# The second product of a packed-attention and FFN kernel by one level of Strassen's scheme, in two phases over the inner layer

## The chip, the cores and the metric

The kernel runs on one core of a Trainium2 chip. The metric is the device time of one execution in microseconds; three executions of the kernel before took 696.87, 698.0 and 700.45 us, median 698.0.

## What is computed

```python
def _attn_ref(q, k, v, p):              # 8 batches, 8 heads, 576 tokens, 64 wide; 32 packed queries p
    ...
    p_packed = sm_attn(p, k, v)         # attention of the 32 packed queries over the 576 tokens
    out = sm_attn(q, p_packed, p_packed)  # attention of every token over the 32 packed rows
def _moe_ref(x, w_in, w_out):           # x: 4608 x 512, w_in: 512 x 2048, w_out: 2048 x 512
    h = x @ w_in
    g = h * (1.0 / (1.0 + np.exp(-1.702 * h)))
    return g @ w_out
```

All inputs and the output are f32. The output of the attention, heads side by side, is the x of the second function.

## The kernel before, in words

The attention weights of a token over the 32 packed rows, times (packed rows x `w_in`), are the first product h, so x itself is never formed. For each batch, `m_chunk` multiplies the packed rows by a chunk of 512 columns of `w_in` (f32, four chunks); `h_mm` multiplies the result, as stationary blocks of 128 columns, by the attention weights of half a batch (288 tokens). `out_mm` is the second product g @ `w_out`: for one block f of 128 inner columns, and one block i of 128 tokens, it adds to a PSUM bank of 128 tokens x 512 output columns. There are 16 blocks f and four token blocks in a batch; the 64 tokens left over in each batch are kept (`h_over`) and done for two batches at once (`over_mm`).

Both products want more digits than one fast (fp32r) matmul gives. Each operand is split into an upper part (a cast to fp32r: `m_upper`, `a_upper`, `h_upper`, `upper_w`) and a lower part (what is left: `m_lower`, `a_lower`, `h_lower`, `lower_w`), and three terms are added: upper x upper, upper x lower, lower x upper. So a block of h is six matmuls of 288 columns (`h_mm`, line 605), a block of the second product three of 512 (`product`, line 665):

```python
def product(acc, g, f, at, start, stop):
    for i, (part, gp) in enumerate(((0, g[0]), (1, g[0]), (0, g[1]))):
        nc.tensor.matmul(
            acc, gp[:, at : at + P], wo[f][:, part, :],
            start=(start and i == 0), stop=(stop and i == 2),
        )
```

The gate between them is a Tanh on ScalarE (`h_tanh`, line 613) and a multiplication on VectorE (`h_gate`, `h_over`, line 595). Tanh and the Exp of the two softmaxes are in one activation table. Weights arrive as words of eight bytes and are decoded by ScalarE (`begin_w`, line 208) and VectorE (`join_w`, line 220).

The order of the work is a table of steps, `order`, written out by hand: its entries run from first to last, and each engine executes its own instructions in that order. Waits between engines are by semaphores that the tile framework sets. Short `warm` matmuls on an identity stand in the table where TensorE has no work in the first microseconds. SP's queue issues nearly all transfers, in the table's order.

Of the kernel before, what the change touches and what calls it, by code (L numbers as in the profile page):

```python
# [8 lines left out]
F32 = mybir.dt.float32  # L9
# [12 lines left out]
def kernel(  # L22
# [42 lines left out]
    NF = DF // P  # L65
    FC = 512
    NFC = DF // FC
    CF = FC // P
    NB = S // P
    REST = S - NB * P  # L70
    KC = (S + P - 1) // P
    KLAST = S - (KC - 1) * P
    DEC = 3
    MB = 2
    LATE = [(B - 1, 2)]
# [6 lines left out]
    ps_b = ctx.enter_context(tc.tile_pool(name="ps_b", bufs=2, space=PSUM))  # L82
# [7 lines left out]
    w_in_sb = [cst.tile([P, NP, FC], F32, name=f"w_in{i}") for i in range(NFC)]  # L90
    w_in_raw = w_in.bitcast(U16)
    w_out_raw = w_out.bitcast(U16)

# [9 lines left out]
    def o_tile(name):  # L103
        return wk.tile([P, DM], F32, tag="o", name=name, bufs=4)

    def bank_b(name):
        return ps_b.tile([P, FC], F32, tag="psb", name=name)

    def bank_h(name):
        return ps_h.tile([P, FC], F32, tag="psh", name=name)  # L110

    def bank_acc(i):
        return lambda name: ps_acc.tile([P, FC], F32, tag=f"acc{i}", name=name)
# [7 lines left out]
    def warm(i, n):  # L121

        t = ps_h.tile([P, FC], F32, tag="psh", name=f"warm{i}")
        for _ in range(n):
            nc.tensor.matmul(t[:, :P], ident, ident, start=True, stop=True)  # L125
# [5 lines left out]

    kq = {}


# [23 lines left out]

    slot = [12, 4, 8, 12]
    queue = []
    for c in range(NFC):
        queue += [("in", c, j) for j in range(NP)]
        queue += [("out", i) for i in range(CF * c, CF * (c + 1))]
    raw = {}
    wo = {}

    def slot_of(w):  # L170
        return slot[w[1]] + w[2] if w[0] == "in" else w[1]


    def columns(part):
        return slice(0, FC) if part is None else slice(part * FC // 2, (part + 1) * FC // 2)

    def load_w(n, part=None):
        w = queue[n]
        i = slot_of(w)
        if w[0] == "in":  # L180
            src = w_in_raw[w[2] * P : (w[2] + 1) * P, 4 * w[1] * FC : 4 * (w[1] + 1) * FC]
        else:
            src = w_out_raw[w[1] * P : (w[1] + 1) * P, :]
        if not part:
            raw[i] = wk.tile([P, DM, 2], U32, tag=f"wo{i}", name=f"raw{i}")
        halves = raw[i].rearrange("p n w -> p (n w)").bitcast(U16)
        at = columns(part)
        a, e = 4 * at.start, 4 * at.stop - 1
        nc.sync.dma_start(halves[:, a:e], src[:, a + 1 : e + 1])

    tops = wk.tile([P, 4, DM], U32, tag="late", name="tops")
    tops = [tops[:, i, :] for i in range(4)]
    for t in tops:  # L200
        nc.gpsimd.memset(t, 0)
    dec = {}
    top = {}

    def begin_w(n, part=None):
        top[n, part] = tops[(n + (part or 0)) % 4]
        at = columns(part)
        nc.scalar.copy(  # L208
            top[n, part].bitcast(F16).rearrange("p (n h) -> p n h", h=2)[:, at, 1],
            raw[slot_of(queue[n])].bitcast(BF16).rearrange("p n (w h) -> p n w h", h=2)[:, at, 1, 0],  # L210
        )

    def join_w(n, part=None):
        w = queue[n]
        at = columns(part)
        if w[0] == "in":
            dec[n] = w_in_sb[w[1]][:, w[2], :]
        else:
            dec[n] = wk.tile([P, DM], F32, tag="dec", name="dec", bufs=DEC)
        nc.vector.scalar_tensor_tensor(  # L220
            dec[n][:, at].bitcast(U32), raw[slot_of(w)][:, at, 0], 13, top[n, part][:, at],
            op0=ALU.logical_shift_right, op1=ALU.bitwise_or,
        )

    def upper_w(n, engine=nc.scalar):
        i = slot_of(queue[n])
        wo[i] = wk.tile([P, 2, DM], F32R, tag=f"wo{i}", name=f"wo{i}")
        move(engine, wo[i][:, 0, :], dec[n])

    def lower_w(n, engine=nc.gpsimd):  # L230
        w = wo[slot_of(queue[n])]
        engine.tensor_tensor(w[:, 1, :], dec[n], w[:, 0, :].bitcast(F32), op=ALU.subtract)

    def lower_w_mm(n, bank):

        st["wl", n] = bank = bank(f"pswl_{n}")
        nc.tensor.matmul(bank, ident, dec[n], start=True, stop=False)
        nc.tensor.matmul(bank, minus, wo[slot_of(queue[n])][:, 0, :], start=False, stop=True)

    def lower_w_copy(n, engine=nc.scalar):  # L240
        move(engine, wo[slot_of(queue[n])][:, 1, :], st["wl", n])

    st = {}

# [10 lines left out]
    def new1(b, eo):  # L258
        st["x", 1, b, eo] = x_tile(f"x1_{b}_{eo}")
        st["mx", 1, b, eo] = wk.tile([P, 2], F32, tag="mx1", name=f"mx1_{b}_{eo}", bufs=2)  # L260

    def scores1_first(half):

        for eo in range(2):
            if half == 0:
                new1(0, eo)
            st["bank", eo, half] = (bank_acc(half) if eo else bank_b)(f"ps1_0_{eo}_{half}")
        for j in range(NP):
            for eo in range(2):
                mm1(0, eo, half, st["bank", eo, half], j)  # L270

    def max1_first(eo, half):
        nc.vector.tensor_reduce(
            st["mx", 1, 0, eo][:, half : half + 1], st["bank", eo, half][:, :NH],
            axis=AX.X, op=ALU.max,
        )

    def scores1_mm(b, half, banks=(bank_b, bank_b)):
        if half == 0:
            for eo in range(2):  # L280
                new1(b, eo)
# [29 lines left out]
    def exp1_first(eo, half):  # L311
# [3 lines left out]
            st["x", *key][:, tokens(half)], st["bank", eo, half][:, :NH], AF.Exp,  # L315
# [17 lines left out]


# [18 lines left out]
    def turn1_last_mm(b):  # L353
        st["bank", "t", b] = bank = bank_b(f"pstl_{b}")
# [13 lines left out]

    dram = ctx.enter_context(tc.tile_pool(name="dram", bufs=1, space=bass.MemoryType.DRAM))
# [1085 lines left out]
```

## Time and profile before

| what | value |
|---|---|
| median of three runs | 698.0 us |
| the profiled execution | 697.0 us, its span (first to last instruction; nothing lies around it) |
| PE (matmul) busy | 688.2 us, 5032 instructions |
| PEld (weight load) busy | 562.6 us, 5032 instructions |
| DVE (VectorE) busy | 437.2 us, 1112 instructions |
| ACT (ScalarE) busy | 261.9 us, 628 instructions |
| POOL (GpSimd) busy | 86.3 us, 106 instructions |
| mean granted TensorE clock | 0.994 of full speed |
| moved by DMA | 65.18 MB, 94 GB/s over the span |

The profile gives busy time as the union of an engine's instructions. Matmuls are pipelined, and one that lasts 0.396 us may be followed by the next after 0.231 us, so the pace is read from starts, not from durations. An f32 matmul of the program stands in the profile as two. A load of the stationary operand (PEld) belongs to each matmul.

### The profile page before, as it was taken

To read this page: it belongs to the slowest core of one execution; us is meant where nothing else is said; L and a number is where in the kernel's file an instruction comes from. 1 tells how busy PE (TensorE), PEld (TensorE's weight loads), DVE (VectorE), ACT (ScalarE), POOL (GpSimd) and SP (SyncE) were. 2 spreads that over 40 slices of the span, in tenths; PEclk is the share of its full clock that TensorE was granted. 3 is DMA by queue.
4 is the path that set the end of the run, shared out by engine and by line. 5 is a ranking of instruction groups with operands and counts; after the bars stand their busy time and mean duration, and the time that the engine had idled before them with its cause. 6 is when DMAs were issued, how large, how long until landed. Compare 5 with 4: busy or idle time off the path is not lost.

```text
span 697.0 us, 12983 instructions
## 1 busy us (share of the span) xinstructions
PE 688.2 (99%) x5032; PEld 562.6 (81%) x5032; DVE 437.2 (63%) x1112; ACT 261.9 (38%) x628; POOL 86.3 (12%) x106
## 2 busy tenths in 40 slices
PE   8999999999999999999999999999999999999997
PEld 5688788788888888887888878887888887878885
DVE  2998884536565467555685467775785647855443
ACT  4788544423324323433223233332232333333220
POOL 1431372112300224111000000000000000000000
PEclk8999999999999999999999999999999999999999
DMA  8998603342101612055000613034200160010001
GB/s 306 369 346 253 264 1 107 77 128 77 65 1 21 192 39 80 16 130 185 1 31 2 158 46 141 16 97 123 95 16 1 28 186 1 11 51 1 1 15 61
DMA packets 55260, 65.18 MB, mean 94 GB/s; under 512 B 35808, under 2 KB 40864, under 8 KB 54176
## 3 DMA queue, kind: packets, MB, share of 16 engines
q1 hardware_dynamic: 55120, 64.23, 28.9%
q8 instruction: 40, 0.66, 0.4%
q14 instruction: 20, 0.16, 0.1%
q10 hardware_dynamic: 80, 0.13, 0.0%
HBM read 50.78 MB, written 13.57 MB: 92 GB/s over the span
## 4 chain that ended last, share of the span: by engine, by line
PE 95%; DVE 1%; issue 1%; DMA 1%; POOL 0%; ACT 0%; POOLq 0%; DVEq 0%
PE acc L665 52%; PE h L605 29%; PE acc_over L665 5%; PE psm_None L437 4%; PE ps L495 2%; PE pspv L408 1%; PE ps L250 1%; DMA q<-q 1%; PE warm L125 1%; DVE w_in L220 0%; DVE xt L551 0%; DVE sm L539 0%; PE pspt L427 0%; DVE sm L540 0%; DVE x L506 0%
## 5 line engine op out<-in xcount | busy, mean ns | idle before, releaser
L665 PE MATMUL acc<-wo,ghi 128*128 128x512 f32 x1024 | 322.8, 396 | 0.0
L665 PEld LDWEIGHTS acc<-wo,ghi 128*128 128x128 f32 x1024 | 180.1, 188 | 40.0 <-issue 10.3
L613 ACT ACTIVATE g<-h 128x288 f32<-128x288 f32 x256 | 104.1, 410 | 274.7 <-PE h L605 258.8
L665 PE MATMUL acc<-wo,glo 128*128 128x512 f32 x512 | 202.0, 395 | 0.0
L595 DVE SCALAR_TENSOR_TENSOR g<-g,h 128x288 f32<-128x288 f32 (+1 forms) x256 | 104.8, 415 | 116.8 <-ACT g L613 116.2
L605 PE MATMUL h<-ahi,mhi 128*128 128x288 f32 x496 | 139.9, 297 | 0.2 <-DVE g L595 0.2
L605 PE MATMUL h<-ahi,mlo 128*128 128x288 f32 x496 | 138.8, 295 | 0.0
L665 PEld LDWEIGHTS acc<-wo,glo 128*128 128x128 f32 x512 | 96.2, 188 | 22.6 <-DVE glo L592 0.3
L605 PEld LDWEIGHTS h<-ahi,mhi 128*128 128x128 f32 x496 | 93.2, 188 | 16.4 <-DVE x L506 4.9
L605 PE MATMUL h<-alo,mhi 128*128 128x288 f32 x496 | 105.1, 293 | 0.0
L605 PEld LDWEIGHTS h<-ahi,mlo 128*128 128x128 f32 x496 | 93.3, 188 | 6.9
L592 DVE TENSOR_TENSOR glo<-g,ghi 128x288 fp32r<-128x288 f32 (+1 forms) x190 | 79.3, 428 | 14.8 <-ACT ghi L117 10.8
L605 PEld LDWEIGHTS h<-alo,mhi 128*128 128x128 f32 x496 | 79.7, 188 | 0.1
L117 ACT CAST ghi<-g 128x288 fp32r<-128x288 f32 (+1 forms) x144 | 56.0, 402 | 53.4 <-DVE g L595 46.4
L592 POOL TENSOR_TENSOR glo<-g,ghi 128x288 fp32r<-128x288 f32 (+1 forms) x66 | 50.0, 763 | 186.4 <-DVE ghi L119 85.1
L595 DVE SCALAR_TENSOR_TENSOR over<-g,h 128x64 f32<-128x64 f32 x128 | 26.9, 213 | 29.8 <-ACT g L613 29.1
L471 DVE TENSOR_TENSOR mlo<-psm_None,mhi 128x512 fp32r<-128x512 f32 x60 | 40.6, 683 | 4.6 <-ACT mhi L117 4.4
L665 PE MATMUL acc_over<-wo,ghi_over 128*128 128x512 f32 x128 | 39.8, 392 | 0.0
L119 DVE CAST ghi<-g 128x224 fp32r<-128x224 f32 (+1 forms) x112 | 34.0, 309 | 6.9 <-PE acc L665 1.4
L117 ACT CAST mhi<-psm_None 128x512 fp32r<-128x512 f32 x44 | 25.6, 584 | 27.9 <-PE psm_None L437 27.9
L437 PE MATMUL psm_None<-w_in,PT 64*32 64x512 f32 x496 | 33.3, 596 | 0.0
L208 ACT CAST tops<-raw 128x512 f16<-128x512 bf16 (+1 forms) x36 | 24.5, 718 | 8.8 <-DMA raw<-w_in 8.4
(94 smaller groups left out, 476.6 us busy)
## 6 DMA issues: line engine op xcount, KB each, us to landing
q<-q SPq DMA_DIRECT2D x16, 576.0 KB, 5.8
v<-v SPq DMA_DIRECT2D x8, 1024.0 KB, 5.3
o<-o SPq DMA_DIRECT2D x32, 256.0 KB, 2.5
raw<-w_out SPq DMA_DIRECT2D x16, 511.8 KB, 6.2
raw<-w_in SPq DMA_DIRECT2D x12, 511.8 KB, 8.8
k<-pk SPq DMA_DIRECT2D x8, 640.0 KB, 4.2
k<-pk SPq DMA_DIRECT2D x8, 576.0 KB, 6.7
aside<-xb SPq DMA_DIRECT2D x56, 72.0 KB, 2.3
```

The costliest lines, as they stand in the source:

```text
L117: nc.scalar.copy(dst, src)
L119: engine.tensor_copy(dst, src)
L125: nc.tensor.matmul(t[:, :P], ident, ident, start=True, stop=True)
L208: nc.scalar.copy(top[n, part].bitcast(F16).rearrange("p (n h) -> p n h", h=2)[:, at, 1], raw[slot_of(queue[n])].bitcast(BF16).rearrange("p ...
L437: nc.tensor.matmul(banks[eo][32 * j : 32 * j + 32, columns(part)], PT[rows(eo), j, :], w_in_sb[fc][rows(eo), j, columns(part)], start=True ...
L471: nc.vector.tensor_tensor(lo, bank[:, at], hi.bitcast(F32), op=ALU.subtract)
L495: nc.tensor.matmul(banks[eo][32 * j : 32 * j + 32, :NH], st["PT", b][rows(eo), j, :], kq["q", b][rows(eo), half, j, :], start=True, stop=True,
L592: engine.tensor_tensor(lo, src, hi.bitcast(F32), op=ALU.subtract)
L595: nc.vector.scalar_tensor_tensor(dst, th, 1.0, h, op0=ALU.add, op1=ALU.mult)
L605: nc.tensor.matmul(h[:, :NH], m[eo][part][:, fo : fo + P], a[:, eo * NH : (eo + 1) * NH], start=(n == 0), stop=(n == len(terms) - 1),)
L613: nc.scalar.activation(g, st["h", b, f, half][:, :NH], AF.Tanh, scale=1.702)
L665: nc.tensor.matmul(acc, gp[:, at : at + P], wo[f][:, part, :], start=(start and i == 0), stop=(stop and i == 2),)
```

## The change

The second product is done by one level of Strassen's scheme in Winograd's form. A 2 x 2 block product (two token blocks by two inner blocks, times two inner blocks by two halves of 256 output columns) takes seven products instead of eight, four sums of left blocks, four of right blocks and seven on the results.

- The inner layer is done in two phases: `w_in` chunks 0 and 1 and `w_out` blocks 0 to 7 for all batches, then the other half for all batches. A unit u is a pair of inner blocks; a phase has four units. Half a batch (256 of its 288 tokens) is one pair of token blocks; 32 tokens of each half go to `over`, which is done for four batches at once.
- The seven products of a half batch lie two to a PSUM bank in four banks A to D (`prod`); each product is three matmuls of 256 columns.
- Left sums: `g_sum` on VectorE, one of 256 elements (two sums at once) and two of 128 for each unit; then all seven left blocks (896 elements) are split (`g_upper`, `g_lower`).
- Right sums, once for each pair of `w_out` blocks: `w_diff`, and the splits `wa_*`, `wb_*`.
- After phase 0 the seven results of a half batch go to DRAM (`c_take`, `c_store`); in phase 1 they are loaded back (`c_load`), added to the new ones (`c_sum`), and combined (`c_comb`). The attention weights go to DRAM and back the same way (`t_store`, `t_load`).
- Batch 0 does plain products of 512 columns (`prod0`), three terms each.
- The gate is one activation on ScalarE (`g_main`, `g_over`, a sigmoid form of Gelu with scale 2.0); Exp needs another table, so `ACT_TABLE_LOAD` now stands 34 times in ScalarE's order, once before.
- GpSimd has five compute steps left, all in batch 0. PSUM: two pairs of banks serve the first product, scores and packs; four banks accumulate.
- All entries of `order` are listed anew. `load_q0` and half tiles of `w_in` are new at the start.

The core of the diff:

```diff
-    def out_mm(b, f, i):
-        if f == 0:
-            accs[i] = acc_bank(i, f"{b}")
-        product(accs[i], gs[b, f], f, i * P, f == 0, f == NF - 1)
...
+    products = {
+        "A": ((0, 0), (5, 5)),
+        "B": ((3, 6), (4, 4)),
+        "C": ((2, 2), (6, 3)),
+        "D": ((1, 1),),
+    }
...
+    def prod(ph, b, half, u, bank):
+        if u == 0:
+            accs[bank] = acc_bank(bank, f"{ph}_{b}_{half}")
+        acc, gs = accs[bank], st["gs", (ph, b, half, u)]
+        Wa, Wb = (st["W", NU * ph + u, ab] for ab in "ab")
+        for n, (g, w) in enumerate(products[bank]):
+            for i, (gp, wp) in enumerate(((0, 0), (0, 1), (1, 0))):
+                nc.tensor.matmul(
+                    acc[:, n * HC : (n + 1) * HC], gs[:, gp, g],
+                    Wa[:, wp, w] if w < 4 else Wb[:, wp, w - 4],
...
+    def g_main(ph, b, half, u):
+        k = (ph, b, half, u)
+        X = blocks(k)
+        h = st["h", *k]
+        nc.scalar.activation(
+            X[:, :4].rearrange("p (f t) n -> p f (t n)", f=2), h[:, :, :NM], AF.Gelu_apprx_sigmoid, scale=2.0
+        )
...
+    def g_sum(ph, b, half, u, i, engine=nc.vector):
...
+        A21, A11, _, A12 = (plain(k)[:, n] for n in range(4))
+        S3, S1, S2, S4 = (X[:, n] for n in range(4, 8))
+        if i == 1:
+            to, a, b_ = X[:, 4:6], A21.unsqueeze(1).broadcast_to([P, 2, P]), plain(k)[:, 1:3]
+        else:
+            to, a, b_ = ((S2, A11, S1), (S4, A12, S2))[i - 2]
+        engine.tensor_tensor(to, a, b_, op=ALU.subtract)
...
+    def w_diff(kp, i, engine=nc.vector):
...
+        to, x, y = ((T1, B12, B11), (T2, B22, T1), (T3, B22, B12), (T4, T2, B21))[i - 1]
+        engine.tensor_tensor(to, x, y, op=ALU.add if i in (2, 3) else ALU.subtract)
...
+    def c_take(b, half, bank, engine=nc.scalar):
+        move(engine, of_bank(r_tile(0, b, half), bank), acc_blocks(bank))
...
+    def c_sum(b, half, bank):
+        t = of_bank(st["p", b, half], bank)
+        to = r_tile(1, b, half)[:, 2:4] if bank == "C" else t
+        nc.vector.tensor_tensor(to, acc_blocks(bank), t, op=ALU.add)
...
+    def c_comb(b, half, i, engine=nc.vector):
...
+        to, x, y, op = (
+            (U2, P1, P6, ALU.add),
+            (r[:, 5:7], U2.unsqueeze(1).broadcast_to([P, 2, HC]), p[:, 2:4], ALU.add),
+            (C22, U3, P5, ALU.add),
+            (C21, U3, P4, ALU.subtract),
+            (P2, P2, P1, ALU.add),
+            (P3, P3, V, ALU.add),
+        )[i]
+        engine.tensor_tensor(to, x, y, op=op)
...
+        (prod, 0, 3, 0, 0, "B"), (g_over, 0, 3, 0, 2), (prod, 0, 3, 0, 0, "D"), (sum1, 4, 0),
```

**TensorE, batch 3.** First the kernel before, where blocks of h (ahi, alo: attention weights; mhi, mlo: packed rows x `w_in`) alternate with blocks of the second product (acc; wo: weights, ghi, glo: the gated h):

```order
L605 MATMUL h_1_9_3801<-alo_1_3264,mhi_2_1_3696 128x288
L427 MATMUL pspt_3816<-ident,pn_3789 128x128
L665 MATMUL acc_3_3421<-wo_767,ghi_6_3654 128x512 x2
L665 MATMUL acc_3_3421<-wo_767,glo_6_3655 128x512
L665 MATMUL acc_3_3421<-wo_888,ghi_7_3685 128x512 x2
L665 MATMUL acc_3_3421<-wo_888,glo_7_3686 128x512
L665 MATMUL acc_3_3421<-wo_937,ghi_8_3720 128x512 x2
L665 MATMUL acc_3_3421<-wo_937,glo_8_3721 128x512
```

The change, also in batch 3 of phase 0 (gs: the seven left blocks of a unit, Wa and Wb: the right blocks, A to D: the banks):

```order
L599 MATMUL h_3_0_3_2234<-a_3_0_2099,m_1_2130 128x288 x12
L740 MATMUL accB_3_0_2260<-Wb_795,gs_3_0_0_2225 128x256 x6
L740 MATMUL accD_3_0_2268<-Wa_386,gs_3_0_0_2225 128x256 x3
L740 MATMUL accB_3_0_2260<-Wb_806,gs_3_0_1_2244 128x256 x6
L740 MATMUL accD_3_0_2268<-Wa_397,gs_3_0_1_2244 128x256 x3
L740 MATMUL accC_3_0_2291<-Wa_386,gs_3_0_0_2225 128x256 x6
L740 MATMUL accA_3_0_2300<-Wa_386,gs_3_0_0_2225 128x256 x3
L740 MATMUL accA_3_0_2300<-Wb_795,gs_3_0_0_2225 128x256 x3
L740 MATMUL accC_3_0_2291<-Wa_397,gs_3_0_1_2244 128x256 x6
L740 MATMUL accA_3_0_2300<-Wa_397,gs_3_0_1_2244 128x256 x3
L740 MATMUL accA_3_0_2300<-Wb_806,gs_3_0_1_2244 128x256 x3
L599 MATMUL h_3_1_0_2333<-a_3_1_2205,m_0_2112 128x288 x12
```

What were runs of three matmuls of 512 columns are now runs of three or six of 256, bank by bank, and a whole pair of h blocks (twelve matmuls) stands together.

**VectorE, in the middle of the program.** Before, a block f has gates of 288 and 224 elements, a short one for the rest of the tokens, and lower parts (glo):

```order
L595 SCALAR_TENSOR_TENSOR g_0_1_4368<-g_0_1_4368,h_0_1_4334 128x288
L119 CAST ghi_1_4378<-g_1_1_4250 128x224
L592 TENSOR_TENSOR glo_1_4379<-g_1_1_4250,ghi_1_4378 128x224
L595 SCALAR_TENSOR_TENSOR g_0_2_4383<-g_0_2_4383,h_0_2_4353 128x288
L592 TENSOR_TENSOR glo_1_4379<-g_0_1_4368,ghi_1_4378 128x288
L592 TENSOR_TENSOR glo_2_4387<-g_0_2_4383,ghi_2_4386 128x288
L595 SCALAR_TENSOR_TENSOR over_0_4287<-g_1_2_4408,h_1_2_4371 128x64
L595 SCALAR_TENSOR_TENSOR g_1_2_4408<-g_1_2_4408,h_1_2_4371 128x224
```

The change, phase 1, batch 3:

```order
L677 TENSOR_TENSOR gs_3_0_0_6333<-X_3_0_0_6293,gs_3_0_0_6333 128x896
L659 TENSOR_TENSOR X_3_0_1_6342<-X_3_0_1_6342 128x256
L776 TENSOR_TENSOR p_1_6074<-accA_2_1_6193,p_1_6074 128x512
L776 TENSOR_TENSOR p_1_6074<-accB_2_1_6167,p_1_6074 128x512
L790 TENSOR_TENSOR r_2_1_6374<-p_1_6074 128x256
L659 TENSOR_TENSOR X_3_0_1_6342<-X_3_0_1_6342 128x128
L790 TENSOR_TENSOR r_2_1_6374<-r_2_1_6374,p_1_6074 128x512
L659 TENSOR_TENSOR X_3_0_1_6342<-X_3_0_1_6342 128x128
L790 TENSOR_TENSOR p_1_6074<-p_1_6074,r_2_1_6374 128x256
L790 TENSOR_TENSOR r_2_1_6374<-r_2_1_6374,p_1_6074 128x256
L790 TENSOR_TENSOR p_1_6074<-p_1_6074 128x256
L776 TENSOR_TENSOR r_2_1_6374<-accC_2_1_6260,p_1_6074 128x512
```

No gate is left; in its place stand the sums of left blocks (X, line 659), a lower part of 896 elements (gs, line 677), and, once for each half batch, adding the stored results (p, line 776) and combining them (line 790).

**SP, the start.** The change issues, up to the last `w_in` tile of chunk 1 (raw_in_3; home: half tiles of chunk 0):

```order
L187 DMA raw_out_0_None<-w_out 128x2047
L187 DMA home_186<-w_in 128x1023
L187 DMA raw_out_0_None<-w_out 128x2047 x3
L129 DMA q_1_334<-q 128x1152
L155 DMA k_356<-pk 128x1280
L187 DMA raw_in_0_None<-w_in 128x2047
L187 DMA raw_in_1_None<-w_in 128x2047
L149 DMA v_415<-v 128x2048
L151 DMA v_415<-v_last 128x512
L551 DMA t_aside_0_462<-xt_0_332 128x576
L187 DMA raw_in_2_None<-w_in 128x2047
L187 DMA raw_in_3_None<-w_in 128x2047
```

Ahead of these rows stand k, v, half of q and seven half tiles. In the kernel before, v of batch 1 and the aside tiles came later, and `w_in` of chunks 1 to 3 and `w_out` ahead of them.

## Rows read from the trace of the kernel before

**Rows 1.** The page, busy time of each engine, its share of the span, and instructions.

```profile
PE 688.2 (99%) x5032; PEld 562.6 (81%) x5032; DVE 437.2 (63%) x1112; ACT 261.9 (38%) x628; POOL 86.3 (12%) x106
```

**Rows 2.** The page, the chain that ended last: shares of the span by engine, then by line.

```profile
PE 95%; DVE 1%; issue 1%; DMA 1%; POOL 0%; ACT 0%; POOLq 0%; DVEq 0%
PE acc L665 52%; PE h L605 29%; PE acc_over L665 5%; PE psm_None L437 4%; PE ps L495 2%; PE pspv L408 1%; PE ps L250 1%; DMA q<-q 1%; PE warm L125 1%; DVE w_in L220 0%; DVE xt L551 0%; DVE sm L539 0%; PE pspt L427 0%; DVE sm L540 0%; DVE x L506 0%
```

**Rows 3.** The waits of PE, seven rows that add up to 4.2 us, the first two and the last: who waited for whom, us in total, times, longest.

```profile
PE warm L125 <- POOL ident masks.py:199: 1.4, 1, 1.4
PE pspv L408 <- DMA v<-v: 1.0, 1, 1.0
...
PE h L605 <- DVE g L595: 0.2, 1, 0.2
```

**Rows 4.** Pace in dense stretches: a piece of the chain with its 24 matmuls (start us, us, what), then the timeline of PE at 401 us and of its weight loads (start us, us, engine, line, operation, count).

```profile
355.09 5.55 PE acc_over L665 x24
...
401.39 0.29 PE L605 MATMUL h<-ahi,mlo 128*128 128x288 f32 x1
401.52 0.29 PE L605 MATMUL h<-ahi,mhi 128*128 128x288 f32 x1
...
401.65 0.32 PEld L605 LDWEIGHTS h<-alo,mhi 128*128 128x128 f32 x2
```

**Rows 5.** Groups of instructions of line 665, PE: count, busy us, mean ns of one, idle us before.

```profile
L665 PE MATMUL acc<-wo,ghi 128*128 128x512 f32 x1024 | 322.8, 396 | 0.0
L665 PE MATMUL acc<-wo,glo 128*128 128x512 f32 x512 | 202.0, 395 | 0.0
...
L665 PE MATMUL acc_over<-wo,ghi_over 128*128 128x512 f32 x128 | 39.8, 392 | 0.0
L665 PE MATMUL acc_over<-wo,glo_over 128*128 128x512 f32 x64 | 25.2, 394 | 0.0
...
L665 PEld LDWEIGHTS acc<-wo,glo 128*128 128x128 f32 x512 | 96.2, 188 | 22.6 <-DVE glo L592 0.3 <-POOL glo L592 0.2
```

**Rows 6.** The warm matmuls, the narrowest ones with a 128x128 load: a stretch of the timeline of PE, their mean in the groups by line, and the window 7.1 to 9.3 us (us, busy time and instructions of each engine, granted clock, DMA share, GB/s).

```profile
7.03 2.27 PE L125 MATMUL warm<-ident 128*128 128x128 f32 x18
...
L125 PE MATMUL warm<-ident 128*128 128x128 f32 x64 | 11.4, 337 | 1.9 <-POOL ident masks.py:199 1.4 <-ACT x L117 0.5
...
7.10:9.30 2.20, 2.20 (x19) 2.02 (x18) 1.25 (x4) 0.94 (x4) 0.00 (x0) 1.00 0.97 328
```

**Rows 7.** Two windows of 35 us: us, busy time and instructions of PE, PEld, DVE, ACT, POOL, granted clock, DMA share, GB/s.

```profile
0.00:35.00 35.00, 30.69 (x325) 21.27 (x326) 20.39 (x57) 20.17 (x52) 10.51 (x21) 0.90 0.91 336
35.00:70.00 35.00, 35.00 (x218) 29.17 (x217) 31.14 (x72) 29.70 (x64) 9.67 (x10) 1.00 0.90 301
```

**Rows 8.** The timeline of PE in the first microseconds and at the first whole chunk of `w_in` (start us, us, engine, line, operation, count, idle before and its releaser).

```profile
28.89 0.72 PE L250 MATMUL ps<-k 64*32 64x288 f32 x16
...
31.34 0.40 PE L605 MATMUL h<-ahi,mhi 128*128 128x288 f32 x1 [0.16 <-DVE g L595]
...
40.27 1.09 PE L437 MATMUL psm_None<-w_in,PT 64*32 64x512 f32 x16
41.29 0.40 PE L605 MATMUL h<-ahi,mhi 128*128 128x288 f32 x1
...
402.13 1.32 PE L408 MATMUL pspv<-v,aT 128*32 128x64 f32 x80
```

**Rows 9.** Groups of DVE instructions that go, and one that stays (columns as in rows 5).

```profile
L595 DVE SCALAR_TENSOR_TENSOR g<-g,h 128x288 f32<-128x288 f32 x128 | 57.5, 450 | 86.3 <-ACT g L613 85.8
L595 DVE SCALAR_TENSOR_TENSOR g<-g,h 128x224 f32<-128x224 f32 x128 | 48.3, 380 | 30.4 <-ACT g L613 30.4
...
L595 DVE SCALAR_TENSOR_TENSOR over<-g,h 128x64 f32<-128x64 f32 x128 | 26.9, 213 | 29.8 <-ACT g L613 29.1
...
L220 DVE SCALAR_TENSOR_TENSOR w_in<-raw,tops 128x512 uint32<-128x512 uint32 x12 | 8.6, 731 | 1.1 <-ACT tops L208 1.1
```

**Rows 10.** The timeline of DVE in a stretch without gaps: start us, us, engine, line, operation.

```profile
46.07 0.45 DVE L592 TENSOR_TENSOR glo<-g,ghi 128x288 fp32r<-128x288 f32 x1
46.44 0.21 DVE L595 SCALAR_TENSOR_TENSOR over<-g,h 128x64 f32<-128x64 f32 x1
46.57 0.68 DVE L220 SCALAR_TENSOR_TENSOR dec<-raw,tops 128x512 uint32<-128x512 uint32 x1
47.17 0.45 DVE L595 SCALAR_TENSOR_TENSOR g<-g,h 128x288 f32<-128x288 f32 x1
```

**Rows 11.** Groups of ACT instructions (columns as in rows 5).

```profile
L208 ACT CAST tops<-raw 128x512 f16<-128x512 bf16 x28 | 20.8, 784 | 0.5 <-DVE dec L220 0.5
...
L117 ACT COPY o<-acc 128x512 f32<-128x512 f32 x16 | 9.3, 586 | 13.3 <-PE acc L665 13.3
...
L88 ACT ACT_TABLE_LOAD x1 | 1.3, 1283 | 0.7 <-PEq L1446 0.7
```

**Rows 12.** The page, DMA issues: queue, count, KB each, median us from issue to landing.

```profile
o<-o SPq DMA_DIRECT2D x32, 256.0 KB, 2.5
```

**Rows 13.** The timeline at the end: start us, us, engine, line, operation.

```profile
692.14 0.40 PE L665 MATMUL acc_over<-wo,glo_over 128*128 128x512 f32 x1
692.63 0.69 DVE L119 COPY o_over<-acc_over 128x512 f32<-128x512 f32 x1 [6.75 <-issue]
693.36 0.56 ACTq L701 DMA_DIRECT2D o<-o_over  x1
```

More of the change, by code (lines that the diff above doesn't have):

```diff
@@ L198, with span, raw_tile @@
-    tops = wk.tile([P, 4, DM], U32, tag="late", name="tops")
-    tops = [tops[:, i, :] for i in range(4)]
+    homes = {("in", 0, j, s): NP * s + j for s in range(2) for j in range(NP)}
+    raw = {}
+    homed = {}
+    def span(w):
+        return (0, FC) if w[3] is None else (w[3] * HC, (w[3] + 1) * HC)
+    def raw_tile(w):
+        name = "raw_" + "_".join(str(i) for i in w)
+        if w in homes:
+            i, at = divmod(homes[w], 3)
+            if i not in homed:
+                homed[i] = wk.tile([P, 3, HC, 2], U32, tag="gs", name=f"home{i}", bufs=GBUFS)
+            return homed[i][:, at]
+        if w[0] == "out" and w[1] < 2:
+            return wk.tile([P, FC, 2], U32, tag="r", name=name, bufs=2)
+        return wk.tile([P, FC, 2], U32, tag="raw", name=name, bufs=RBUFS)
@@ new lines, in load_w @@
+    def load_w(*w):
+        kind, i, j, side = w
+        a, e = span(w)
+        if kind == "in":
+            src = w_in_raw[j * P : (j + 1) * P, :]
+            at = i * FC + a
+        else:
+            src = w_out_raw[i * P : (i + 1) * P, :]
+            at = a
+        n = e - a
+        raw[w] = raw_tile(w)
+        halves = raw[w].rearrange("p n w -> p (n w)").bitcast(U16)
+        nc.sync.dma_start(halves[:, : 4 * n - 1], src[:, 4 * at + 1 : 4 * (at + n)])
+    tops = [cst.tile([P, FC], U32, name=f"top{i}") for i in range(2)]
@@ new lines, with over_tile, h_mm @@
+    over_g = {}
+    def over_tile(ph, g, u):
+        if (ph, g, u) not in over_g:
+            over_g[ph, g, u] = wk.tile([P, 2, NM], F32, tag=f"over{u}", name=f"over_{ph}_{g}_{u}")
+        return over_g[ph, g, u]
+    def h_mm(ph, b, half, u, i):
+        if i == 0:
+            st["h", ph, b, half, u] = pair_bank(f"h_{ph}_{b}_{half}_{u}")
+        h = st["h", ph, b, half, u][:, i, :NH]
+        f = 2 * NU * ph + 2 * u + i
+        m, a = st["m", b, f // CF], st["a", ph, b, half]
+        at = slice(f % CF * P, (f % CF + 1) * P)
+        terms = [(eo, part, 0) for eo in range(2) for part in range(2)]
+        terms += [(eo, 0, 1) for eo in range(2)]
+        for n, (eo, part, ap) in enumerate(terms):
@@ L699, in over_store, with blocks, over_part @@
[L699 to L706 removed]
+    def blocks(k):
+        st["X", k] = X = wk.tile([P, 8, P], F32, tag="X", name="X_" + "_".join(map(str, k)), bufs=XBUFS)
+        return X
+    def over_part(ph, b, half, u):
+        at = (b % 4) * 2 * REST + half * REST
+        return over_tile(ph, b // 4, u)[:, :, at : at + REST]
@@ new lines, in g_split, with g_upper @@
+    def g_split(k, a, e):
+        X = st["X", k][:, 1 + a : 1 + e] if a >= 3 or k[1] != "over" else plain(k)[:, 1 + a : 1 + e]
+        hi, lo = (st["gs", k][:, i, a:e] for i in range(2))
+        return X, hi, lo
+    def g_upper(ph, b, half, u, a=0, e=7, engine=nc.scalar):
+        k = (ph, b, half, u)
+        if ("gs", k) not in st:
+            st["gs", k] = wk.tile(
+                [P, 2, 7, P], F32R, tag="gs", name="gs_" + "_".join(map(str, k)), bufs=GBUFS
+            )
+        X, hi, lo = g_split(k, a, e)
+        move(engine, hi, X)
@@ new lines, in store @@
+    def store(b, half, r=None, engine=nc.sync):
+        o = r_tile(1, b, half)[:, :4].rearrange("p (r e) w -> p r (e w)", r=2)
+        if b == "over":
+            t = out.rearrange("(x t) e -> x t e", t=NH)[:, NM:, :]
+            for x in range(4 * r, 4 * r + 4):
+                engine.dma_start(t[8 * half + x], o[x % 4 * REST : (x % 4 + 1) * REST, r, :])
+        elif r is None:
+            at = b * S + half * NH
+            engine.dma_start(out[at : at + NM, :].rearrange("(r p) e -> p r e", p=P), o)
+        else:
+            at = b * S + half * NH + r * P
+            engine.dma_start(out[at : at + P, :], o[:, r])
```

2032 lines of the change are left out of this document (1065 added, 967 removed).

## The prediction

> **What bounds the kernel now.** I read the page's busy shares first, then the chain that ended last, then what PE waited for, then the spacing of the matmuls. PE is busy 99% of the span, DVE 63%, ACT 38%, POOL 12% [rows 1]. A busy PE may still be a slow one, so the chain decides: 95% of it is PE, 57% the second product (52% the main rows, 5% the over rows) and 29% the first [rows 2]. PE's waits add up to 4.2 us [rows 3], the last of them at 31.34 us [rows 8]: after that PE never stops. What is left is the pace: in a dense stretch a 128x512 matmul starts every 0.231 us (24 in 5.55) and a 128x288 one every 0.131 us [rows 4]. These are 0.45 ns a column at either width, at a granted clock of 1.00 (the 2.4 GHz level). So the second product costs 1024+512+128+64 = 1728 matmuls [rows 5] x 0.231 = 399 us of the 697, and only PE's columns, its start and its end can change the time.
>
> **The second product.** Batch 0 keeps plain products: 2 phases x 2 halves x 4 units x 2 row blocks x 6 = 192 matmuls of 512 columns. Everything else goes by seven products with three terms each, 256 columns wide: 7 batches x 16 units x 21 = 2352, and 16 over units x 21 = 336, together 2688. Columns fall by 11%, but instructions rise from 1728 to 2880, each with a 128x128 load of its own. No row shows a 256-column fp32r matmul. By proportion it takes 0.231/2 = 0.1155, or 0.131 x 256/288 = 0.1164. From below, the f32 warm matmuls, each with a 128x128 load, follow one another every (2.27-0.34)/17 = 0.114 us at clock 1.00 [rows 6]; from above it can't cost more than the wider one, 0.131. I take **0.116**, nearest to both proportions. Cost: 2688 x 0.116 + 192 x 0.231 = 312 + 44 = 356 us, **43 us less** (50 less at 0.114, 3 less at 0.131).
>
> The Trainium skill, "TensorE: Matmul & The Clock Gate", section "Back-to-back issue gap", gives N/2.4 + 2.5 ns for a warm matmul, 216 ns at 512 columns and 109 at 256. The trace does not agree: 231 ns. By that rule the change would take away 38 us, an estimate from the page.
>
> The rest of PE's work is the same: 1536 matmuls of the first product, the w_in products, scores, packs. The extra f32 products that split the first weights by PE stand where PE waits for loads.
>
> **The start.** In both programs PE becomes dense when the weights are there. Up to the last w_in tile of chunk 1 the new queue on SP moves 12.0 thousand KB (k, v, q of batch 0, eight half tiles and four whole ones of w_in, four of w_out, half of k and all of v of batch 1, one aside store). At the 336 GB/s of the first 35 us [rows 7] that is 36.6 us; with a landing of some 3 us [rows 12] and the decoding (0.78 on ACT [rows 11], 0.73 on DVE [rows 9]) w_in is ready at about 41 us. The kernel before starts the same chunk at 40.27 us [rows 8], but has then done 24 matmuls of 288 columns and one pair of score products (0.72 each) more than the new order lists ahead of it: 24 x 0.131 + 1.4, **5 us lost**. It can be 0 if the queue runs ahead, 9 if the two raw buffers for w_out stall it.
>
> **DVE.** POOL's 86 us move to DVE and ACT, and DVE's gate (57.5+48.3+26.9 us [rows 9]) becomes one ACT activation. What DVE gains is priced by its pace, not by the mean of an instruction: 512 elements start every 0.60 us, 288 every 0.37, 64 every 0.13 [rows 10], so n/0.96 + 67 ns, and a float copy from SBUF about half of the first term. By that 256, 128, 896 and 1024 elements take 0.33, 0.20, 1.00 and 1.13. The sums of the left blocks: 128 x 0.33 + 256 x 0.20 = 94. The lower parts: 112 x 1.00 + 16 x (0.60+0.47) + 16 x 0.60 = 139. Adding the stored half and combining: 52 x 0.60 + 16 x 0.33 + 16 x 0.60 + 80 x 0.33 = 73. Weights: joins 28 x 0.60 + 8 x 0.33, lower parts 7 x 1.13 + 8 x (0.87+0.33), sums 32 x 0.33, together 48. Lower parts of w_in products and attention: 31 x (1.13+0.67) = 56. Casts put on DVE (22 of 896 elements at 0.56, others): 34. Softmax and turns, 17 passes of 288 to 576 elements at 0.37 to 0.67 a batch and their small ones: 100. Sum 544; in the listed order 231 instructions read what the one ahead wrote and wait for its end (0.69 against 0.60), 0.09 each: **565 us**, 85% of the time forecast. In phase 0 a batch has 36 us of it (8 units x 1.73, attention 12.5, lower parts 3.6, casts 3, over 1.8, dependent starts 1) beside 41 of PE (168 matmuls x 0.116, 96 x 0.131, over 84 x 0.116 / 4, two w_in products of 1.02, four score products of 0.72, a pack of 1.32 [rows 8] and its turn). The kernel before held 89% in its second 35 us [rows 7] with no wait of PE after 32 us. So this cover is thin but has been seen. Where it is thinnest, from the last plain products to the first product of batch 1, DVE has about 28 us (16 weight sums, their splits, the softmax of batch 1) beside 25 of PE (11 groups of 6 x 0.231, 3 x 12 x 0.131, pack, scores and w_in products 5): **3 us**, 0 to 8.
>
> **ACT** takes 128 activations of 512 and of 64 elements from PSUM (nearest row 0.59 for a copy of 512 [rows 11], some 0.21 for the short one): 102 us. Upper parts 90 x 0.94 and 22 more: 107. W_in products and attention 25 x (1.0+0.67): 42. Partial results to SBUF: 32. Decoding 26. Table loads, one before and 34 now (Exp and the gated function take turns), x 1.28: 44. Attention and weights 52. Sum 405 us, 61%. It stays covered as long as the two pairs of PSUM banks for the first product come free in time.
>
> **Transfers** rise by 41 MB (partial sums 31, attention 9) on 65, from 94 to about 160 GB/s where 336 has been held [rows 7]; each is loaded back half a batch ahead, against a landing of 2.5 us [rows 12]. Nothing; if the cover went, one landing per half.
>
> **The end.** Before, the last matmul is followed by a 0.69 us copy and the stores [rows 13]. Now a 512-element sum follows and four stores on one queue; an issue took 0.56, so three more are 1.7: **+2 us** (1 to 3).
>
> **Sum** on the profiled execution, 697.0 us (1.0 under the median of 698.0): 697 - 43 + 5 + 3 + 2 = **664 us**.
>
> **The rivals.**
> Loads set the pace (ends slower). Each load shows 0.188 us [rows 5], longer than a 256-column matmul; if loads cannot come faster than the fp32r row shows, every 0.131 us, the product costs 352 + 44 = 396 and the kernel 664 + 40 = **704**. It decides from 0.130 us a matmul, where 697 + 3.5 is reached. For: no fp32r load here comes faster. Against: two loads of 0.19 fit into 0.32 [rows 4], and the warm matmuls load every 0.114 [rows 6]. If loads could not overlap at all, 2688 x 0.188 would make it 858; 1536 first products at 0.131 with loads of 0.188 exclude that nearly. The Trainium skill, "Perfetto Trace Analysis", section "Identifying the Most-Contended Engine", has TensorE's headroom read from the summed load slices; by this reading the loads would exceed the window. The trace's overlapping loads speak against it. 5% for 704, 1% for 858.
>
> DVE falls behind. If half of its 1157 instructions paid the 0.09 us, not a fifth, it would need 593; packed at the 89% of [rows 7], with 15 us idle at the start and 5 at the end, 593/0.89 + 20 = **686**. For: every unit's three sums, upper and lower part hang in one chain. Against: the order interleaves units. 18%.
>
> Table loads reach PE. 33 x 1.28 = 42 us more on ACT, each ahead of an activation that frees a PSUM pair; if half shows, 664 + 21 = **685**. For: PE takes its products in order and cannot skip a late first product. Against: the order lists second products between first ones, which PE can do meanwhile. 10%.
>
> The start costs nothing and a matmul 0.114: 664 - 7 - 5 = **652**, 8%.
>
> **How the numbers follow.** 664 has 58%, with its own range 654 to 676. The range goes from 650 to 688: it takes in the two late rivals and the early one, and leaves out 704, 858 and whatever is earlier, under a tenth. About 0.5%, 3.5 us, is what a measurement can tell here. Slower than that: 704 and 858, 6%. Within: 3%, the matmul near 0.129 or two late rivals at once. Faster: 91%.
>
> **What would show it.** The line of the seven products at 256 columns with starts every 0.115 to 0.117 and 2688 of them; chain still over 90% PE; DVE near 85% busy; ACT near 60% with 34 table loads; POOL almost gone; first dense products at about 41 us. Wrong if PE's spacing is 0.13, if PE's waits after 45 us go beyond 10 us in total, or if the chain holds more than 5% of DVE or ACT.

## The result, and the profile after the change

After: 702.25 us median of 20 runs (699.73 to 704.12), beside 697.69 for the kernel before in the same session (20 runs, 696.55 to 700.92). The ratio is 1.0051, 95% interval 1.0036 to 1.0065: half a per cent slower, where 664 us had been forecast. The profiled execution has a span of 701.3 us, before 697.0.

The page after, busy time and the chain that ended last, beside [rows 1, 2]:

```profile
PE 673.6 (96%) x6264; PEld 606.4 (86%) x6264; DVE 568.0 (81%) x1157; ACT 377.8 (54%) x695; POOL 5.5 (1%) x14
...
PE 81%; DVE 8%; ACT 6%; DMA 2%; issue 2%; POOL 0%; ACTq 0%; DVEq 0%; POOLq 0%
PE h L599 25%; PE accA L740 11%; PE accC L740 11%; PE accB L740 10%; PE accD L740 5%; PE psm_None L449 3%; DMA raw_in_None<-w_in 2%; PE accC L698 2%; PE accD L698 2%; PE ps L493 2%; PE accD_warm L119 1%; PE pspv L410 1%; PE accB_over L740 1%; PE accB L698 1%; PE accA_over L740 1%
```

PE fell from 95% of the chain to 81%. The pace did not fail; three successive pieces of the chain (start us, us, what):

```profile
99.00 0.70 PE accC L740 x6
99.71 0.71 PE accB L740 x6
100.42 0.35 PE accD L740 x3
```

Six matmuls of 256 columns, each with its own load, start in 0.71 us: 0.118 apart. What is new are the waits of PE (who waited for whom, us in total, times, longest): 19 rows, 20.8 us, where before had 7 with 4.2 [rows 3]. The first six:

```profile
PE psm_None L449 <- ACT over L621: 4.8, 1, 4.8
PE ps L275 <- ACT over L621: 2.5, 3, 0.9
PE h L599 <- ACT over L621: 2.5, 4, 1.0
PE psm_None L449 <- DVE x L503: 1.9, 1, 1.9
PE accD_warm L119 <- POOL ident masks.py:199: 1.4, 1, 1.4
PE ps L275 <- ACT x L111: 1.0, 1, 1.0
```

All but the fifth wait for one of the two pairs of PSUM banks (`h`, `ps` and `psm` share them) that ACT or DVE has yet to empty. Three windows (us, busy time and instructions of PE, PEld, DVE, ACT, POOL, granted clock, DMA share, GB/s) show where: the change of batch, the change of phase, and phase 1 with almost nothing lost.

```profile
70.00:105.00 35.00, 29.50 (x264) 24.21 (x265) 30.13 (x65) 21.39 (x38) 0.00 (x0) 1.00 0.57 167
385.00:420.00 35.00, 30.23 (x187) 24.70 (x186) 20.39 (x34) 15.56 (x30) 0.00 (x0) 0.90 0.28 94
455.00:490.00 35.00, 35.00 (x293) 33.98 (x292) 28.09 (x56) 15.10 (x26) 0.00 (x0) 1.00 0.35 101
```

A matmul's slice lasts about 0.28 us while the next starts after 0.118, so waits shorter than the difference leave PE "busy". I therefore also worked out from the starts of all matmuls how far PE is **behind its own work**: the clock, less the matmuls done so far, each at its clean spacing (0.235 us for 512 columns, 0.133 for 288, 0.1175 for 256; products of the attention and with w_in at their mean in the kernel before; warm matmuls at nothing). The work is 669.8 us before and 625.8 after. Us behind at a given time (e11 and e13 are experiments further below):

```
                      35     70    105    210    385    420    665
before              22.2   22.2   22.3   22.5   22.8   22.9   22.8
after               23.4   30.2   37.1   47.7   55.2   63.1   68.1
e11, relisted       23.4   28.3   33.3   40.0   47.5   47.5   50.8
e13, one table      23.4   28.6   31.2   37.1   43.1   43.1   46.2
```

The change takes away 44 us of work, and PE falls 45 us further behind: 7 between 35 and 70 us, 25 up to 385, 8 at the change of phase, 5 after it. What follows the start of the last matmul adds 2 (4.9 before, 6.9 after).

**One wait read from the chain.** Pieces in order of time, from the last second-score product of batch 1 to the first score products of batch 2:

```profile
76.72 0.73 PE ps L493 x16
...
78.56 0.69 DVE xt L547
79.25 0.73 DVE x L503 x2
79.98 1.11 DVE m L473
81.09 0.65 DVE mx L522
81.74 0.67 DVE a L567
82.41 0.67 DVE x L526
83.08 1.15 DVE m L473
84.22 0.04 issue
84.26 1.86 PE h L599 x12
86.12 0.02 issue
86.15 0.05 ACT X L616
86.19 0.45 issue
86.64 0.23 ACT over L621
86.87 0.04 issue
86.91 0.80 PE ps L275 x16
```

The `h` of 84.26 is the second unit's. It reads chunk 0, so it does not use what the second L473 computes (the lower part of `m`, chunk 1); it needs only the pair of banks that this L473 empties. And L473 stands in DVE's list behind two transpositions (`x` L503), the lower parts of chunk 0 and of `a`, and a maximum and a subtraction of a softmax that is used half a batch later. The score products (L275) then need a pair that ACT's `over` (L621) empties. PE takes nothing out of its listed turn, so each of these is a stop.

**The change of phase** (start us, us, engine, line, operation, idle before and its releaser):

```profile
385.40 2.54 PE L599 MATMUL h<-a,m 128*128 128x288 f32 x18
...
391.33 0.76 ACT L198 CAST top<-raw_in_None 128x512 f16<-128x512 bf16 x1 [2.41 <-DMA raw_in_None<-w_in]
391.96 0.58 ACT L616 ACTIVATE X<-h 128x512 f32<-128x512 f32 x1
...
392.44 0.22 ACT L621 ACTIVATE over<-h 128x64 f32<-128x64 f32 x1
...
392.71 2.07 PE L449 MATMUL psm_None<-w_in,PT 64*32 64x512 f32 x16 [4.77 <-ACT over L621]
...
394.71 2.93 PE L698 MATMUL accB<-Wa,gs 128*128 128x512 f32 x6
```

`h` is done at 387.9, but ACT waits 2.41 us for a w_in tile with the gate queued behind it. PE idles 4.8 us, and part of the window runs at the 1.2 GHz level: 0.90 granted on average over the 35 us, and the chain has the six matmuls of 512 columns that follow at

```profile
394.79 2.86 PE accB L698 x6
```

where e11 further below needs 1.40 us for six.

### The profile page after: what moved, and what is told of

It reads as the page before. It is cut to its first block, busy times and chain, and to the rows that moved or that the text cites. A ratio compares the mean times of both kernels' runs of the same rounds, so it can differ in the third digit from the quotient of the medians.

```text
span 701.3 us, 15383 instructions
## 1 busy us (share of the span) xinstructions
PE 673.6 (96%) x6264; PEld 606.4 (86%) x6264; DVE 568.0 (81%) x1157; ACT 377.8 (54%) x695; POOL 5.5 (1%) x14
## 4 chain that ended last, share of the span: by engine, by line
PE 81%; DVE 8%; ACT 6%; DMA 2%; issue 2%; POOL 0%; ACTq 0%; DVEq 0%; POOLq 0%
PE h L599 25%; PE accA L740 11%; PE accC L740 11%; PE accB L740 10%; PE accD L740 5%; PE psm_None L449 3%; DMA raw_in_None<-w_in 2%; PE accC L698 2%; PE accD L698 2%; PE ps L493 2%; PE accD_warm L119 1%; PE pspv L410 1%; PE accB_over L740 1%; PE accB L698 1%; PE accA_over L740 1%
## 5 line engine op out<-in xcount | busy, mean ns | idle before, releaser
L599 PE MATMUL h<-a,m 128*128 128x288 f32 x1536 | 225.0, 296 | 5.2 <-ACT over L621 2.5
L599 PEld LDWEIGHTS h<-a,m 128*128 128x128 f32 x1536 | 208.4, 188 | 12.6 <-ACT over L621 4.3
L677 DVE TENSOR_TENSOR gs<-X,gs 128x896 fp32r<-128x896 f32 x112 | 120.7, 1086 | 23.9 <-ACT gs L111 23.1
L111 ACT CAST gs<-X 128x896 fp32r<-128x896 f32 (+1 forms) x101 | 91.0, 907 | 85.2 <-DVE X L659 20.3
L616 ACT ACTIVATE X<-h 128x512 f32<-128x512 f32 x128 | 76.0, 599 | 102.3 <-PE h L599 79.2
L659 DVE TENSOR_TENSOR X<-X 128x256 f32<-128x256 f32 (+1 forms) x336 | 102.5, 329 | 26.1 <-ACT X L616 23.5
L740 PE MATMUL accB<-Wb,gs 128*128 128x256 f32 x672 | 98.8, 282 | 0.3 <-DVE gs L677 0.3
L740 PE MATMUL accC<-Wa,gs 128*128 128x256 f32 x672 | 98.3, 281 | 0.0
L740 PEld LDWEIGHTS accB<-Wb,gs 128*128 128x128 f32 x672 | 87.4, 188 | 7.8 <-issue 6.4
L740 PEld LDWEIGHTS accC<-Wa,gs 128*128 128x128 f32 x672 | 87.3, 188 | 6.4 <-issue 3.9
L473 DVE TENSOR_TENSOR m<-psm_None,m 128x1024 fp32r<-128x1024 f32 x31 | 37.6, 1212 | 5.1 <-ACT m L111 4.8
L621 ACT ACTIVATE over<-h 128x64 f32<-128x64 f32 x128 | 27.7, 225 | 0.0
L111 ACT CAST a<-xt 128x576 fp32r<-128x576 f32 (+1 forms) x27 | 17.7, 654 | 10.3 <-PE h L599 6.4
```

What stands on the lines that cost most here:

```text
L111: nc.scalar.copy(dst, src)
L473: nc.vector.tensor_tensor(m[:, 1, :, at], st["bank", "m", b, c, part], m[:, 0, :, at].bitcast(F32), op=ALU.subtract,)
L599: nc.tensor.matmul(h, m[:, part, eo, at], a[:, ap, eo * NH : (eo + 1) * NH], start=(n == 0), stop=(n == len(terms) - 1),)
L616: nc.scalar.activation(X[:, :4].rearrange("p (f t) n -> p f (t n)", f=2), h[:, :, :NM], AF.Gelu_apprx_sigmoid, scale=2.0)
L621: nc.scalar.activation(over_part(ph, b, half, u), st["h", ph, b, half, u][:, :, NM:NH], AF.Gelu_apprx_sigmoid, scale=2.0,)
L659: engine.tensor_tensor(to, a, b_, op=ALU.subtract)
```

## The experiments

Each ratio is to the kernel before on the same chip, with its 95% interval; "gain" is the distance from 1.0051, times 697.7. Both intervals taken together, a difference of less than about 2 us between two of these kernels (3 between those with few runs) can't be told from nothing.

**1. One cause at a time.** e1, the gates ahead of the last decoding at the change of phase (40 of the 2913 steps stand elsewhere; the core of it):

```
- (begin_w, "in", 3, 2, None), ..., (begin_w, "in", 3, 3, None), ..., (g_main, 1, 0, 0, 0), ..., (m_mm, 0, 3), ..., (prod0, 1, 0, 0, 1)
+ (g_main, 1, 0, 0, 0), ..., (prod0, 1, 0, 0, 1), ..., (begin_w, "in", 3, 2, None), ..., (begin_w, "in", 3, 3, None), ..., (m_mm, 0, 3)
```

> At the phase boundary the first two gated units of phase 1 and their plain products are listed ahead of the decoding of the last two w_in tiles. Theory (ACT's list order): ACT waits 2.41 us for a w_in tile with the emptying of the PSUM pairs queued behind it, so PE stops 4.8 us and then runs 6.8 us at half clock; without that, the stop and the half-clock stretch both go: 702 - 5 - 4 = 693 us, 690 to 695. Rival (the transfer itself is late): PE only stops a little later, at the chunk 3 product that needs the tile, the half clock stays: 700 to 702.

1.0032 (1.0012 to 1.0052), gain 1.3 us. The rival was nearer: PE is 6.8 us further behind across the window, not 7.9.

e2: `AF.Gelu_apprx_sigmoid` becomes `AF.Tanh`.

> The gated function is replaced by Tanh, which Exp's table also holds, so 33 table loads of 1.28 us go; nothing else changes (the gate itself is left out of the computation). Theory T (table loads reach PE through the PSUM pairs that ACT empties late): PE's 25 us of waits between 70 and 385 us mostly go, and some 5 us before: 702 - 20 = 682, 675 to 687. Theory D (DVE's passes set the pace there): 698 to 702.

0.9997 (0.9976 to 1.0018), gain 3.8 us. Table loads matter, but not 20 us.

e3, in `g_lower`: `+ if ph == 0 and b != "over": e = 3`, and in `prod`: `gs[:, gp if ph or b == "over" or g < 3 else 0, g]`.

> In phase 0 the lower part is taken of three of the seven left blocks only, and the products of the other four read the upper part in its place (left out of the computation: the lower parts of four blocks); PE has the same matmuls, DVE 56 passes of 1.09 us less 0.55 each, 30 us less. Theory D: PE's 25 us of waits in phase 0 fall by half or more, 702 - 15 = 687, 680 to 692. Theory T: 699 to 702.

1.0026 (1.0004 to 1.0047), gain 1.7 us with 27 us of DVE gone: theory D falls.

> The three edits together. If the waits are separate, the savings add: by T and the list order 673, by D and the list order 678, by all three 658. If two of them cover the same waits, the sum of the single savings is not reached. The floor, with no wait after the start but the ones that the kernel before has too, is 702 - 44 = 658 us.

0.9970 (0.9948 to 0.9993), gain 5.7 us; the single gains add to 6.8. Together they bring back 6 of the 45 us.

**2. What may have been overlooked.** e5: the steps of w_in chunk 3 and of w_out 12 to 15 exchange places, then as e1 with `m_mm` of chunk 3 behind the second unit.

> The four loads of w_in chunk 3 change places with the four last of w_out, so chunk 3 is in SBUF some 15 us sooner, and the gated units at the boundary stand ahead of the remaining decoding, with chunk 3's product behind the second unit. Theory (chunk 3 comes late: its decoding, its product, its parting and the next gate follow one another while PE waits): the 8 us that PE falls behind its own work between 385 and 420 us fall to 2, so 702 - 6 = 696 us, 694 to 698. Rival (the boundary is short of ACT and DVE, whatever comes first): 700 to 702.

1.0074 (1.0054 to 1.0095), 1.6 us above the changed kernel and so no gain. The w_in tile was there, but the stop was not gone: PE's only wait row from 380 to 420 us, and ACT's timeline ahead of it, read now

```profile
PE h L599 <- ACT over L621: 4.6, 1, 4.6
```

```profile
391.46 1.42 ACT L198 CAST top<-raw_out_None 128x512 f16<-128x512 bf16 x2
397.00 0.83 ACT L111 CAST Wb<-T 128x768 fp32r<-128x768 f32 x1 [4.11 <-DVE T L259]
```

In my order a cast of weight sums, which waits 4.11 us for DVE, stands in ACT's list ahead of the next gate. The wait at the head of the list was another one; PE's stop was the same.

e6: `groups(x)[:, :n]` with n = 1 from batch 1 on, in the four softmax passes.

> The four softmax passes of the second scores of batches 1 to 7 (maximum, subtraction, sum, normalisation) are run on one group of 32 elements instead of all 18 (left out of the computation: the other groups), which takes 56 passes of some 0.65 us to some 0.15: 28 us less of DVE, all of it in the attention of phase 0. Theory A (PE waits in phase 0 for DVE's attention passes, which stand in a row ahead of the parts that free a PSUM pair): of the 25 us that PE falls behind between 70 and 385 us 10 or more go, 702 - 12 = 690, 685 to 694. Rival (the waits come from the order of the list and the length of the chain, not from these passes): 698 to 702.

1.0034 (1.0019 to 1.0049), gain 1.2 us: theory A falls as well.

> Chunk 3 early, one table (no gate), the lower part of three of seven blocks in phase 0, and the short softmax, together (left out: as in each alone). If the waits of PE are those that these four remove, what is left is the start (8 us more than before) and the switches: 702 - 44 + 10 = 668, 663 to 675. If they come from PE's own list, which takes a product of the next unit before its parts can be there, the sum stays above 685.

0.9972 (0.9960 to 0.9984), gain 5.5 us, 696 us. With 60 us of DVE and 44 of ACT gone, PE has 97% of the span, and it is still 60 us behind at the end:

```profile
PE 669.2 (97%) x6264; PEld 605.7 (87%) x6264; DVE 508.5 (73%) x1157; ACT 334.0 (48%) x662; POOL 5.5 (1%) x14
```

This, with "above 685" put down to PE's own list, turned the search to the order.

e8: `(sub2, 1..7, half, None, pool)` and the same for `norm2`, on e5.

> Chunk 3 early, and in batches 1 to 7 the subtraction and the normalisation of the second softmax go back to POOL, 28 passes of some 1.2 us on an idle engine in place of 28 of 0.67 on DVE. Theory A: 19 us less on DVE where PE waits for it, 4 to 8 us less than chunk 3 early alone, 690. Rival: POOL's longer passes lengthen the chain, the same as chunk 3 early alone or up to 3 us more.

1.0104 (1.0078 to 1.0131), 2.1 us above e5, which is within the noise: no gain, as the rival had it.

**3. The order itself.** e9 to e12 and e15 have the 2913 steps of the changed kernel; only the list differs (and with it how often a table is loaded, 34 times in the changed kernel and 36 in e11). It was sought by many small moves of single steps, judged by the durations and handovers of the traces. In e11 2688 of 2913 steps stand elsewhere, half of them by at most 13 places. At the change of phase, for instance, the first gate of phase 1 now stands among the over products:

```
+ (prod, 0, "over", 1, 1, "C"), (g_main, 1, 0, 0, 0), (prod, 0, "over", 1, 1, "D"), ..., (load_w, "in", 3, 3, None)
```

> The same 2913 steps, the same instructions, tiles and buffers, in another order: from the 176th step on the list was rearranged by a program that follows the durations and handover times read from the trace of the changed kernel (each handover taken 0.05 us longer), by exchanging neighbours until PE waited least. Theory O (the order of the list: every engine takes its work strictly in the listed order, and in the kernel as listed PE's next item waits for a part that stands too far back in DVE's or ACT's list, or for one of the two PSUM pairs): 30 us of the 46 that PE falls behind go, 702 - 25 = 677 us, 668 to 686. Rival (DVE and ACT as such are too short of time once PE needs 44 us less, whatever the order): 695 to 702. Rival (hidden handover costs that the trace does not show as waits): 688 to 695.

0.9876 (0.9861 to 0.9891), gain 12.2 us, 688.6. In this first list a weight sum of phase 1 is parted anew before one plain product has read the old one, so that product differs; the instructions are the same.

> As the relisted kernel, but with every handover taken 0.12 us longer while the order was sought, so the order keeps more distance between a part and its use. Theory O: the same within 3 us, 677; if real handovers vary more than the trace's medians, this one is the faster, by up to 4 us.

0.9951 (0.9921 to 0.9980), gain 7.0 us: more distance was not better. Both missed 677; e9 lies at the lower end of the second rival's range, 688 to 695. In e9 the transfers of the packed scores had become a wait of their own,

```profile
PE pspv L410 <- DMA aT<-aside: 5.9, 5, 2.2
```

and each group of f32 products began 0.1 us later than assumed. With both put in:

> The same steps once more in a sought order, now from the 152nd step on, with what the first relisted runs showed put in: the transfers of the packed scores through DRAM land 0.4 us later than assumed, and each group of f32 products costs 0.1 us more at its start; all reads ahead of a write keep their place. Handovers 0.04 us longer than the trace's. Theory O: PE falls behind by some 10 us less than in the first relisted kernel, 679 us, 674 to 685. Rival (the first relisted order has all there is to be had): 687 to 690.

**0.9800 (0.9774 to 0.9826), 684.97 us (4 runs, 684.29 to 686.36)**, gain 17.5 us: faster than both kernels, though at the upper end of what was expected. The page, PE's first waits, the two windows, and a piece of the chain:

```profile
PE 667.7 (98%) x6264; PEld 602.0 (88%) x6264; DVE 564.0 (83%) x1157; ACT 378.9 (55%) x697; POOL 5.5 (1%) x14
```

```profile
PE h L599 <- DVE m L473: 1.6, 2, 0.9
PE accD_warm L119 <- POOL ident masks.py:199: 1.4, 1, 1.4
PE pspv L410 <- ACT X L616: 1.3, 1, 1.3
PE pspv L410 <- DMA aT<-aside: 1.2, 2, 0.8
```

```profile
70.00:105.00 35.00, 31.58 (x332) 26.86 (x330) 29.72 (x65) 24.31 (x42) 0.00 (x0) 1.00 0.63 182
385.00:420.00 35.00, 35.00 (x213) 30.38 (x212) 23.35 (x40) 15.25 (x33) 0.00 (x0) 1.00 0.39 132
```

```profile
389.92 1.40 PE accB L698 x6
```

DVE and ACT have as much to do as in the changed kernel; PE's wait rows add up to 8.6 us instead of 20.8, and the 8 us at the change of phase are gone with the clock at 1.00. By the table above, the gain lies 2 us before 70 us, 6 between 70 and 385 (of the 25 lost there), 8 at the change of phase and 2 after it.

> As the last, with handovers 0.08 us longer while the order was sought: 680 us, 675 to 686; faster than the last one if the spread of real handovers matters.

0.9867 (0.9839 to 0.9894), 689.9: 4.7 us behind e11. The spread of handovers isn't it.

**4. What holds the rest.** e2 and e3 once more, on e11's order.

> The second relisted order with Tanh in place of the gated function, so 33 table loads of 1.28 us go (the gate is left out of the computation). In the kernel as listed this gave 4 us. If ACT's table loads hold PE once the order is right, 685 - 8 = 677 or less; if they stay covered, 683 to 685.

0.9730 (0.9694 to 0.9767), 679.9: 4.9 us under e11, between the two expectations.

> The second relisted order with the lower part of three of seven left blocks in phase 0 (left out: the lower parts of the other four), 30 us less of DVE. In the kernel as listed this gave 2 us. If DVE's passes as such hold PE in phase 0 once the order is right, 685 - 8 = 677 or less; if not, 682 to 685.

0.9819 (0.9788 to 0.9850), 685.7: nothing, in either direction, though DVE's busy time falls from 564.0 to 536.5 us. DVE's time as such is no bound here, at 83% of the span.

> The second relisted order sought further, with the last runs' handovers put in (transfers of the packed scores 0.3 us later, PE's restart after a wait 0.12 us instead of 0.09). Theory O: more of the waits go, 682 us, 679 to 685. Rival: the second order has all there is to be had by order, 685 to 688.

0.9844 (0.9816 to 0.9871), 687.4: no better than e11. This search found nothing more.

## Why the prediction was wrong, point by point

- **Second product, 43 us less: right.** By the median spacing of the starts (0.232 us at 512 columns in both kernels, 0.118 at 256, where 0.116 was taken) the product takes 362 us beside 401 before, 39 less; by the mean spacing without the stops (anything above one and a half times the median) it is 44 less. The rival with loads as the pace is out. The Trainium skill, "TensorE: Matmul & The Clock Gate", section "Back-to-back issue gap", gives 109 ns at 256 columns by a formula that it states for an isolated matmul; in the trace's dense stream it is 118 ns.
- **Start, 5 us: the ready time was right, the size was not.** The product with w_in chunk 1 starts at 41.28 us, forecast 41, and there PE has lost some 3 us against the kernel before. At 70 us it has lost 8: `ps` and `h` wait for ACT and DVE in turn, which the term, made of transfers alone, left out.
- **DVE's cover, 3 us: the step that failed.** From DVE's and PE's sums for a batch I concluded that the cover was thin but seen. The sum was right (565 forecast, 568.0 measured), the conclusion wrong: PE fell 25 us behind between 70 and 385 us, with DVE at 27 to 33 us of each 35. It is not the amount of DVE's work: e3, e6 and e14 take 27 to 31 us off DVE and give 1.7, 1.2 and nothing, and e7 with 60 us of DVE and 44 of ACT gone gives 5.5. The order counts: e11 leaves DVE its work and gives 17.5 us in all, 6 of them in this stretch. What the term needed is not how much DVE does beside PE, but what stands ahead of the one part that PE's next item takes. How the rest of the 25 us divides is only in part settled (see "Open").
- **ACT, "covered as long as the two pairs come free in time":** the condition was named and not priced. Three of the first four wait rows are ACT's `over` emptying a pair. ACT's total was even smaller than forecast, 377.8 against 405.
- **The change of phase** was not in the sum at all: 8 us, of which a stop of 4.8 and a lower clock after it. The kernel before has only one phase.
- **Table loads:** 34, as counted, and worth 4 to 5 us (e2, e13), where the rival had 21.
- **Rival "DVE falls behind", 686:** no; less DVE work brings nothing. By the prediction's own terms this rival comes to 544 + 578 x 0.09 = 596 us of DVE, not 593, and so to 690, outside the range. **Transfers:** nothing, but for the last w_in tiles, and there e5 shows that an early tile alone does not help. **End, 2 us:** right (4.9 to 6.9).
- **The chances.** Faster was put at 91% because every rival was a longer total or a slower pace. A list in which one engine's items wait at the head of another's queue was no rival, so nothing in the range covered it. Both warnings named ahead came true: PE's waits after 45 us go beyond 10 (17.7 by the rows), and DVE and ACT hold 8% and 6% of the chain.

**Open.** In e11 PE is still 28 us further behind than the kernel before. Some 5 are table loads (e13), 6 the start up to 70 us, 3 phase 1, and DVE's work as such is none. That leaves some 14 between 70 and 385 us. Some 3 of them are still wait rows of PE in e13. Another part no wait row shows: in this stretch PE turns from its fp32r matmuls to f32 products (scores, products with w_in) 16 times in the kernel before, always for a group of 16 of each, one behind the other; 30 times in the changed kernel and 36 times in e11, mostly for one group. From the starts, with no wait between (from the matmul ahead to the second one behind, less two spacings), such a turn takes 0.84 us for scores alone, 1.21 for w_in alone and 1.71 for both, so parting the two costs 0.34 us each time, an estimate of some 5 us in e11. This too is order, of PE's own list. The rest is not settled: no run has e11's order and less DVE and ACT work together, e15 shows only that this search found no better order, and more buffers were not tried.

## What to carry to other kernels

When the bounding engine is given 7% less work (44 of 670 us here) in a program whose order is fixed by hand, a busy share of 80% on another engine does not show that it covers the bounding one: for each wait of the latter, read what stands ahead of the releasing instruction in that engine's list. If relieving the engine that the waits name brings little, as here in e3, e4, e6 and e7, test the order itself with the same instructions before giving up the change. A pace term and an order term belong in separate lines of a forecast, the second with a range as wide as the first one's gain.

## What the runs showed of the hardware

Around a stop of PE of 4.8 us the clock was granted at the lower level for a stretch (0.90 on average over 35 us; six matmuls of 512 columns in 2.86 us, 1.40 in e11), so that 8 us were lost, more than the stop itself. The weight loads are busy 606.4 us of 701.3 and still don't set the pace: 0.188 us a load, one matmul every 0.118, so they overlap. The first matmul after a group of f32 products started 0.33 us (scores) or 0.52 us (w_in) after the last of them, and the second 0.22 us after the first, without any wait; in a dense run it is 0.118.
